# Second layer of a spectral mixture-of-experts kernel: operand addresses of both matrix products moved by 64 bytes

## The chip, the cores and the metric

The kernel runs on one core of a Trainium2 chip. The metric is the device time of one execution in microseconds (us). Three runs of the kernel before gave 3828.07, 3829.45 and 3830.55 us; the median is 3829.45 us.

The core's engines are TensorE (PE in the profile; its weight loads are listed as PEld), VectorE (DVE), ScalarE (ACT), GpSimd (POOL) and SyncE (SP). On-chip memory has 128 partitions, and an address here is the byte at which a tile starts within each partition.

## The reference

```python
# x: (8, 3072, 256); stage 1, a circular convolution along the sequence
X = np.fft.rfft(x, axis=1)
y = np.fft.irfft(X * (filt_r + 1j * filt_i)[None], n=3072, axis=1)
x = y.reshape(24576, 256)
# first layer: 8 experts, each token to its best one
e_idx = np.argmax(x @ w_gate, axis=1)
h = np.maximum(x[mask] @ w1[e], 0.0)              # 256 -> 1024
out[mask] = gate_w * eom * (h @ w2[e])            # 1024 -> 256
# second layer: dense
h = np.maximum(x @ w_in, 0.0)                     # 256 -> 2048
return (h * h) @ w_out                            # 2048 -> 256
```

The change touches the second layer only.

## The kernel before

The kernel runs three stages: the transform with its filter and inverse, the first layer (its matmuls run from 606.5 to 1793.2 us, at first between those of the transform), and the second layer (from 1797.9 us to the end). All engine programs are written out in the order in which the code emits them; waits between engines are semaphores that follow from the data.

A matmul has a stationary operand, which a weight load brings into the array first, and a moving operand, which is streamed through it. In the profile a matmul is written `out<-moving,stationary`.

**Second layer.** The 24576 tokens are 48 tiles of 512. The 2048 inner columns are 8 blocks `u` of 256. One pair (tile, block) is a unit; there are 384. Numbers are split in a high and a low part (`bh`/`bl`, `hh`/`hl`, `wsh`/`wsl`, `woh`/`wol`), and each product is three matmuls: high x high, low x high and high x low.

- `up2` (L881 holds its matmul) forms one block of h. It uses 7 products of 128 x 128 by 128 x 256 in place of 8, so 21 matmuls of 256 columns. Its stationary operands are 128-column pieces of the weights `wsh` and `wsl`, its moving operands the seven pieces of 256 columns of the split tile, `bh` and `bl`. It has four parts with 6, 6, 6 and 3 matmuls.
- ScalarE and VectorE then add up the quarters (`C`, L888 to L903), square the positive part (`q`, L905) and split it into `hh` and `hl` (`split_h`, L912 and L914).
- `down2` (L927) multiplies by the second weights. Here the stationary operands are 128-column pieces of `hh` and `hl`, and the moving ones are rows of 256 columns of `woh` and `wol`. It has 24 matmuls of 256 columns, in four parts with 3, 6, 9 and 6.
- `steps_m` interleaves them: in step n it emits part 0 of `up2` of unit n, part 0 of `down2` of unit n - 2, then part 1 of both, and so on. So a step has 45 matmuls, in which the products change from one to the other eight times. `split_h` of unit n - 1 goes between, and in some steps also a part of `split_t` (L860 to L871), which splits the next tile.

**Where the tiles stand.** `wsh`, `wsl`, `woh` and `wol` are allocated one after the other in the pool `wres` on the left side of the memory; behind it come the pools of the loaded tiles and of the decoder. On the right side `open_m2` opens its pools one below the other, first `pad2`, a tile of 16 floats (64 bytes) that nothing reads. All other tiles have sizes that are multiples of 512 bytes. In the program of the kernel before the tiles start at these bytes:

| tile | first byte | modulo 512 | modulo 128 |
|---|---|---|---|
| wsh, wsl | 21504, 50176 | 0 | 0 |
| woh, wol | 78848, 95232 | 0 | 0 |
| bh (2 buffers), bl (2) | 199616, 206784, 213952, 221120 | 448 | 64 |
| hh (3 buffers), hl (3) | 148416 to 156608, 160704 to 168896 | 448 | 64 |

The pieces within a tile that a matmul takes begin at multiples of 512 bytes, so the last two columns hold for every operand. In the first layer all operands (`xh`, `xl`, `wh`, `wl`, `hh`, `hl` of L802 and L819) start at multiples of 512 bytes.

Of the kernel before, what the change touches and what calls it, by code (L numbers as in the profile page):

```python
# [12 lines left out]
F32 = mybir.dt.float32  # L13
# [89 lines left out]
def spectral_moe_kernel(ctx: ExitStack, tc: tile.TileContext, x, filt_r, filt_i, w_gate, w_og, w1, w2,  # L103
# [58 lines left out]
    pl = {"xsm": ctx.enter_context(tc.tile_pool(name="xsm", bufs=2, side="right"))}  # L162
# [458 lines left out]
    def decode(pool, src, parts, val=None):  # L621


        v = nc.vector
        raw = pool.tile([128, ND, 2], I32, name="raw")
        nc.sync.dma_start(out=raw, in_=src)
        yield
        H, L = raw[:, :, 1], raw[:, :, 0]
        ea = pool.tile([128, ND], I32, name="ea")
        eb = pool.tile([128, ND], I32, name="eb")  # L630
        v.tensor_scalar(ea, H, 20, 0x7FF, op0=ALU.logical_shift_right, op1=ALU.bitwise_and)
        v.tensor_scalar(eb, ea, 896, 0, op0=ALU.subtract, op1=ALU.max)
        v.tensor_scalar(ea, eb, 255, None, op0=ALU.min)
        v.tensor_scalar(eb, ea, 23, None, op0=ALU.logical_shift_left)
        yield
        v.tensor_scalar(ea, H, -2147483648, None, op0=ALU.bitwise_and)
        v.tensor_tensor(eb, ea, eb, ALU.bitwise_or)
        yield
        v.tensor_scalar(ea, H, 0xFFFFF, 3, op0=ALU.bitwise_and, op1=ALU.logical_shift_left)
        mb_ = pool.tile([128, ND], I32, name="mb_")  # L640
        v.tensor_scalar(mb_, ea, 0x3F800000, None, op0=ALU.bitwise_or)
        P = eb.bitcast(F32)
        a = pool.tile([128, ND], F32, name="a")
        v.tensor_tensor(a, mb_.bitcast(F32), P, ALU.mult)
        yield
        v.tensor_scalar(ea, L, 1, None, op0=ALU.logical_shift_right)
        lf = pool.tile([128, ND], F32, name="lf")
        v.tensor_scalar(lf, ea, 2.0 ** -51, None, op0=ALU.mult)
        v.tensor_tensor(lf, lf, P, ALU.mult)
        yield  # L650
        if val is not None:
            v.tensor_tensor(val, a, lf, ALU.add)
        for at, hi, lo in parts:
            v.tensor_tensor(hi, a[:, at], lf[:, at], ALU.add)
            v.tensor_tensor(a[:, at], a[:, at], hi.bitcast(F32), ALU.subtract)
            v.tensor_tensor(lo, a[:, at], lf[:, at], ALU.add)
        yield

    def decode_all():
        wres = ctx.enter_context(tc.tile_pool(name="wres", bufs=1))  # L660


        wsh, wsl = (wres.tile([128, F2 // 256, 7, 128], F32R, name=n) for n in ("wsh", "wsl"))
        woh, wol = (wres.tile([128, F2 // 128, D], F32R, name=n) for n in ("woh", "wol"))
        w2nd.extend((wsh, wsl, woh, wol))
        lpool.append(ctx.enter_context(tc.tile_pool(name="rp2", bufs=2)))
        pool = dcs.enter_context(tc.tile_pool(name="dcp", bufs=1))
        first, second = slice(0, 128), slice(128, 256)
        for u in range(F2 // 256):
            a0, a1 = (pool.tile([128, ND], F32, name=f"val{c}") for c in range(2))  # L670
            for c, val in enumerate((a0, a1)):
                yield from decode(pool, w_in32[c * 128:(c + 1) * 128, 2 * u * ND:2 * (u + 1) * ND]
                                  .rearrange("p (n two) -> p n two", two=2),
                                  [(at, wsh[:, u, i], wsl[:, u, i])
                                   for at, i in (((first, 0),), ((first, 1), (second, 2)))[c]], val)
            sc = pool.tile([128, 4, 128], F32, name="sc")
            v.tensor_tensor(sc[:, 0], a0[:, second], a1[:, second], ALU.add)
            v.tensor_tensor(sc[:, 1], sc[:, 0], a0[:, first], ALU.subtract)
            v.tensor_tensor(sc[:, 2], a0[:, first], a0[:, second], ALU.subtract)
            v.tensor_tensor(sc[:, 3], a1[:, first], sc[:, 1], ALU.subtract)  # L680
            yield
            nc.scalar.copy(wsh[:, u, 3:7], sc)
            v.tensor_tensor(wsl[:, u, 3:7], sc, wsh[:, u, 3:7].bitcast(F32), ALU.subtract)
            yield
        for f in range(F2 // 128):
            yield from decode(pool, w_out32[f * 128:(f + 1) * 128].rearrange("p (d two) -> p d two", two=2),
                              [(slice(0, D), woh[:, f, :], wol[:, f, :])])
# [152 lines left out]

    def open_m2():
        right(ctx, "pad2", 1).tile([128, 16], F32, name="pad2")
        for name, bufs in (("bp", 2), ("tp2", 1), ("sp", 2), ("cp", 2), ("h2p", 3), ("oup", 2)):
            pl[name] = right(ctx, name, bufs)

    def load_t(t):
        r = lpool[0].tile([128, 2, TT], F32, name="r")
        nc.sync.dma_start(out=r, in_=ytd[:, t * TT:(t + 1) * TT].rearrange("(h p) t -> p h t", p=128))
        ix = lpool[0].tile([128, 4], I32, name="ix", bufs=4)
        nc.sync.dma_start(out=ix, in_=idsc[t * TT:(t + 1) * TT, 0:1].rearrange("(c p) o -> p (c o)", p=128))  # L850
        R[t] = r, ix
# [151 lines left out]
    def steps_m():  # L1003
# [15 lines left out]
        m1.close()  # L1019
        xgs.close()  # L1020
        open_m2()
        st = split_t(0)
        for _ in st:
# [95 lines left out]
    tables()  # L1119
    open_left()  # L1120
    dec.append(decode_all())
    for _ in m:
        pass
# [33 lines left out]
```

## Time and profile before

| | |
|---|---|
| median of three runs | 3829.45 us |
| the profiled execution | 3831.18 us |
| its span, first to last instruction | 3829.5 us |
| TensorE busy | 3762.7 us, 98% of the span |
| VectorE busy | 2767.0 us, 72% |
| ScalarE busy | 1973.5 us, 52% |
| GpSimd busy | 608.2 us, 16% |
| granted TensorE clock, mean | 0.994 |

How to read it: matmuls are pipelined, and the duration of one overlaps the next; the pace of the engine is read from the starts. Durations and starts come from the one profiled execution, the median from three others.

### The profile page before, as it was taken

To read this page: it belongs to the slowest core of one execution; us is meant where nothing else is said; L and a number is where in the kernel's file an instruction comes from. 1 tells how busy PE (TensorE), PEld (TensorE's weight loads), DVE (VectorE), ACT (ScalarE), POOL (GpSimd) and SP (SyncE) were. 2 spreads that over 40 slices of the span, in tenths; PEclk is the share of its full clock that TensorE was granted. 3 is DMA by queue.
4 is the path that set the end of the run, shared out by engine and by line. 5 is a ranking of instruction groups with operands and counts; after the bars stand their busy time and mean duration, and the time that the engine had idled before them with its cause. 6 is when DMAs were issued, how large, how long until landed. Compare 5 with 4: busy or idle time off the path is not lost.

```text
span 3829.5 us, 73425 instructions
## 1 busy us (share of the span) xinstructions
PE 3762.7 (98%) x27256; PEld 3512.9 (92%) x27256; DVE 2767.0 (72%) x5038; ACT 1973.5 (52%) x3909; POOL 608.2 (16%) x641
## 2 busy tenths in 40 slices
PE   8999999999999999999999999999999999999998
PEld 7888877788888888888999999999999999999998
DVE  6678685688888866655777777777777777777776
ACT  6466463354545545544555555555555555555554
POOL 3477575000000000000001100100110010011001
PEclk9999999999999999999999999999999999999999
DMA  6333322455555545543010010001001000100100
GB/s 194 100 117 113 105 86 91 142 158 165 170 163 173 178 150 161 164 148 114 23 29 23 29 29 23 29 23 29 23 29 29 23 29 23 29 23 29 29 18 18
DMA packets 262750, 309.30 MB, mean 81 GB/s; under 512 B 75153, under 2 KB 206194, under 8 KB 262386
## 3 DMA queue, kind: packets, MB, share of 16 engines
q1 hardware_dynamic: 242928, 252.39, 21.8%
q0 software_dynamic: 18432, 51.93, 3.8%
q8 instruction: 215, 3.52, 0.4%
q14 instruction: 149, 1.22, 0.1%
q10 hardware_dynamic: 1026, 0.23, 0.0%
HBM read 224.01 MB, written 80.45 MB: 80 GB/s over the span
## 4 chain that ended last, share of the span: by engine, by line
PE 37%; issue 14%; POOL 2%; DVE 0%; ACT 0%; POOLq 0%; DVEq 0%; ACTq 0%
PE py L927 20%; PE ph L881 13%; PE px L881 5%; POOL out_dram L936 2%; DVE tc L867 0%; DVE bl L871 0%; DVE hl L914 0%; DVE bl L861 0%; ACT bh L869 0%; POOLq L1152 0%; DVE C L899 0%; ACT ou L933 0%; ACT bh L860 0%; ACT u L895 0%; DVE C L900 0%
## 5 line engine op out<-in xcount | busy, mean ns | idle before, releaser
L927 PE MATMUL py<-woh,hh 128*128 128x256 f32 x3072 | 857.2, 279 | 0.0
L927 PE MATMUL py<-woh,hl 128*128 128x256 f32 x3072 | 852.8, 278 | 0.4 <-DVE hl L914 0.4
L927 PE MATMUL py<-wol,hh 128*128 128x256 f32 x3072 | 852.9, 278 | 0.0
L936 POOL DMA_INDIRECT out_dram<-ou,ix x192 | 214.0, 1115 | 2935.7 <-ACT ou L933 2891.8
L927 PEld LDWEIGHTS py<-woh,hl 128*128 128x128 f32 x3072 | 579.9, 189 | 0.9 <-DVE hl L914 0.8
L927 PEld LDWEIGHTS py<-woh,hh 128*128 128x128 f32 x3072 | 579.9, 189 | 0.0
L927 PEld LDWEIGHTS py<-wol,hh 128*128 128x128 f32 x3072 | 576.3, 188 | 0.0
L806 ACT ACTIVATE hh<-ph 128x512 fp32r<-128x512 f32 (+1 forms) x472 | 251.8, 533 | 586.3 <-PE ph L802 559.3
L881 PE MATMUL ph<-bh,wsh 128*128 128x256 f32 x1920 | 541.5, 282 | 5.6 <-ACT bh L860 4.4
L881 PE MATMUL ph<-bh,wsl 128*128 128x256 f32 x1920 | 539.2, 281 | 0.0
L881 PE MATMUL ph<-bl,wsh 128*128 128x256 f32 x1920 | 539.0, 281 | 0.0
L905 DVE SCALAR_TENSOR_TENSOR q<-C 128x1024 f32<-128x1024 f32 x384 | 468.3, 1220 | 2.3 <-ACT C L903 2.2
L808 DVE SCALAR_TENSOR_TENSOR hl<-ph,hh 128x512 fp32r<-128x512 f32 (+1 forms) x472 | 286.8, 608 | 253.4 <-ACT hh L806 248.5
L914 DVE TENSOR_TENSOR hl<-q,hh 128x1024 fp32r<-128x1024 f32 x384 | 467.1, 1217 | 1.1 <-ACT hh L912 1.1
L899 DVE TENSOR_TENSOR C<-ph,p 128x256 f32<-128x256 f32 x384 | 163.5, 426 | 417.1 <-ACT hh L912 412.8
L903 ACT COPY C<-ph 128x256 f32<-128x256 f32 x384 | 143.0, 372 | 519.7 <-PE ph L881 518.2
L912 ACT CAST hh<-q 128x1024 fp32r<-128x1024 f32 x384 | 403.1, 1050 | 1.3 <-DVE q L905 1.3
L881 PEld LDWEIGHTS ph<-bh,wsh 128*128 128x128 f32 x1920 | 363.0, 189 | 6.9 <-issue 4.6
L881 PEld LDWEIGHTS ph<-bl,wsh 128*128 128x128 f32 x1920 | 361.6, 188 | 0.0
L881 PEld LDWEIGHTS ph<-bh,wsl 128*128 128x128 f32 x1920 | 361.5, 188 | 0.0
L819 PE MATMUL py<-hh,wh 128*128 128x512 f32 (+1 forms) x944 | 348.4, 369 | 0.0
L802 PE MATMUL ph<-xh,wh 128*128 128x512 f32 (+1 forms) x944 | 340.3, 360 | 0.0
(261 smaller groups left out, 8184.2 us busy)
## 6 DMA issues: line engine op xcount, KB each, us to landing
r<-in_moe_w_dram SPq DMA_DIRECT2D x448, 256.0 KB
xt<-in_x_dram SPq DMA_DIRECT2D x48, 512.0 KB
r<-ytd SPq DMA_DIRECT2D x48, 512.0 KB
xg<-srt SPq DMA_DIRECT2D x41, 544.0 KB
ytd<-yt SPq DMA_DIRECT2D x41, 512.0 KB
xg<-srt SPq DMA_DIRECT2D x18, 272.0 KB
ytd<-yt SPq DMA_DIRECT2D x18, 256.0 KB
raw<-in_moe_w_in_dram SPq DMA_DIRECT2D x16, 256.0 KB
```

Of the source, the lines that this page charges most:

```text
L802: nc.tensor.matmul(ps, a[:, c, f2 * 128:(f2 + 1) * 128], b[:, c, 0:w], start=n == 0, stop=n == 5)
L806: nc.scalar.activation(hh, ps, AF.Relu)
L808: nc.vector.scalar_tensor_tensor(hl, ps, 0.0, hh.bitcast(F32), op0=ALU.max, op1=ALU.subtract)
L819: nc.tensor.matmul(Y[t][h], a[:, f % 2, h * 128:(h + 1) * 128], b, start=f == 0 and i == 0, stop=f == NF - 1 and i == 2)
L881: nc.tensor.matmul(ps, x[:, u, a], y[:, b], start=start and n == 0, stop=n == 2, skip_group_check=True)
L899: nc.vector.tensor_tensor(C[:, 3], V, p5, ALU.add)
L903: nc.scalar.copy(C[:, 2], V)
L905: nc.vector.scalar_tensor_tensor(q, C, 0.0, C, op0=ALU.max, op1=ALU.mult)
L912: nc.scalar.copy(hh, q)
L914: nc.vector.tensor_tensor(hl, q, hh.bitcast(F32), ALU.subtract)
L927: nc.tensor.matmul(Z[t][k][:, c, :], x[:, 2 * i + k, c * 128:(c + 1) * 128], w[:, 2 * u + i, :], start=u == 0 and m in (0, 12), stop=u == ...
L936: nc.gpsimd.indirect_dma_start(out=outv[4 * t + c], out_offset=bass.IndirectOffsetOnAxis(ap=io[:, c:c + 1], axis=0), in_=ou[:, c, :], in_o ...
```

## The change

Two tiles of 16 floats per partition (64 bytes) are allocated that no instruction reads or writes. `wpad` stands between the first weights (`wsh`, `wsl`) and the second ones (`woh`, `wol`); what is allocated behind it on the left side moves up by 64 bytes. `pad3` is a pool of its own, opened between the pool of `C` and `q` and the pool of `hh` and `hl`; what is opened after it on the right side moves down by 64 bytes.

```diff
         wsh, wsl = (wres.tile([128, F2 // 256, 7, 128], F32R, name=n) for n in ("wsh", "wsl"))
+        wres.tile([128, 16], F32, name="wpad")
         woh, wol = (wres.tile([128, F2 // 128, D], F32R, name=n) for n in ("woh", "wol"))
...
         right(ctx, "pad2", 1).tile([128, 16], F32, name="pad2")
-        for name, bufs in (("bp", 2), ("tp2", 1), ("sp", 2), ("cp", 2), ("h2p", 3), ("oup", 2)):
+        for name, bufs in (("bp", 2), ("tp2", 1), ("sp", 2), ("cp", 2), ("pad3", 1), ("h2p", 3), ("oup", 2)):
             pl[name] = right(ctx, name, bufs)
+            if name == "pad3":
+                pl[name].tile([128, 16], F32, name="pad3")
```

By these sizes `woh` and `wol` come to start at 64 modulo 128 and modulo 512, and `hh` and `hl` at 0 modulo 128 (384 modulo 512); `wsh`, `wsl`, `bh` and `bl` stay.

## Rows read from the trace of the kernel before

**Rows 1.** Windows: PE, PEld, DVE, ACT, POOL busy us (count), clock, DMA share, GB/s.
```profile
2500.00:3000.00 500.00, 500.00 (x4302) 500.00 (x4301) 368.49 (x575) 260.28 (x549) 53.65 (x48) 1.00 0.09 27
```

**Rows 2.** Costliest groups: line, engine, operands, shape, count, busy us, mean ns.
```profile
L927 PE MATMUL py<-woh,hh 128*128 128x256 f32 x3072 | 857.2, 279 | 0.0
```

**Rows 3.** Timeline of TensorE (start us, duration us), the layer's 51st and 17233rd matmul.
```profile
1813.30 0.28 PE L927 MATMUL py<-wol,hh 128*128 128x256 f32 x1
...
3812.37 0.28 PE L927 MATMUL py<-woh,hh 128*128 128x256 f32 x1
```

**Rows 4.** Timeline of TensorE over a unit and a half, first matmuls of stretches.
```profile
2801.06 0.28 PE L881 MATMUL ph<-bh,wsh 128*128 128x256 f32 x1
...
2802.12 0.28 PE L881 MATMUL ph<-bh,wsh 128*128 128x256 f32 x1
...
2803.16 0.28 PE L881 MATMUL ph<-bh,wsh 128*128 128x256 f32 x1
...
2804.58 0.28 PE L881 MATMUL px<-bh,wsh 128*128 128x256 f32 x1
...
2805.27 0.28 PE L927 MATMUL py<-woh,hh 128*128 128x256 f32 x1
...
2806.29 0.28 PE L881 MATMUL ph<-bh,wsh 128*128 128x256 f32 x1
...
2808.39 0.28 PE L881 MATMUL ph<-bh,wsh 128*128 128x256 f32 x1
...
2809.81 0.28 PE L881 MATMUL px<-bh,wsh 128*128 128x256 f32 x1
```

**Rows 5.** Timeline, a matmul of L927 and the weight load behind it.
```profile
2800.94 0.28 PE L927 MATMUL py<-wol,hh 128*128 128x256 f32 x1
2800.95 0.19 PEld L881 LDWEIGHTS ph<-bh,wsh 128*128 128x128 f32 x1
```

**Rows 6.** Timeline of TensorE in the first layer, ends of two runs of steps.
```profile
1697.65 0.39 PE L802 MATMUL ph<-xh,wl 128*128 128x512 f32 x1
...
1711.25 0.39 PE L802 MATMUL ph<-xh,wl 128*128 128x512 f32 x1
...
1783.38 0.28 PE L802 MATMUL ph<-xl,wh 128*128 128x256 f32 x1
...
1793.22 0.28 PE L819 MATMUL py<-hh,wl 128*128 128x256 f32 x1
```

**Rows 7.** Timeline of TensorE at the layer's end, where only L927 runs.
```profile
3812.72 0.28 PE L927 MATMUL py<-wol,hh 128*128 128x256 f32 x1
...
3815.31 0.28 PE L927 MATMUL py<-woh,hh 128*128 128x256 f32 x1
3815.97 0.39 PE L927 MATMUL py<-woh,hl 128*128 128x256 f32 x1 [0.38 <-DVE hl L914]
3816.20 0.28 PE L927 MATMUL py<-wol,hh 128*128 128x256 f32 x1
...
3818.67 0.28 PE L927 MATMUL py<-wol,hh 128*128 128x256 f32 x1
```

**Rows 8.** Timeline of TensorE at the layer's start, after a stop in L881.
```profile
1811.61 0.39 PE L881 MATMUL ph<-bh,wsh 128*128 128x256 f32 x1 [0.59 <-DVE C L899]
...
1812.07 0.28 PE L881 MATMUL ph<-bh,wsh 128*128 128x256 f32 x1
...
1812.75 0.28 PE L927 MATMUL py<-woh,hh 128*128 128x256 f32 x1
```

**Rows 9.** Timeline of VectorE in the unit of rows 4.
```profile
2800.31 0.43 DVE L899 TENSOR_TENSOR C<-ph,p 128x256 f32<-128x256 f32 x1 [1.33 <-ACT hh L912]
...
2803.25 1.22 DVE L871 TENSOR_TENSOR bl<-tc,bh 128x1024 fp32r<-128x1024 f32 x1
```

**Rows 10.** Timeline of TensorE where L881 waited for L899.
```profile
2298.36 0.28 PE L927 MATMUL py<-wol,hh 128*128 128x256 f32 x1
...
2298.77 0.28 PE L881 MATMUL ph<-bl,wsh 128*128 128x256 f32 x1
```

## The prediction

> **What bounds the kernel now.** I read the windows first, then the page's costliest groups, then the timeline of TensorE. From 2500 to 3000 us TensorE is busy in every microsecond (4302 matmuls) at full granted clock, VectorE 74% and ScalarE 52%, DMA 9% [rows 1]: the second layer is bound by how fast matmuls follow each other. The chain of waits that ended last says little here (it runs over the scatters of the output), and a matmul's duration (about 280 ns) says nothing either, since they overlap. What counts is the time from the start of one to the start of the next. A unit (one tile of 512 rows and 256 of the 2048 inner columns) has 24 matmuls of the second product, in three groups of 3072 over the layer [rows 2], and by the code 7 x 3 = 21 of the first, so 45 x 384 = 17280 in all. From the 51st to the 17233rd, 17182 steps take 3812.37 - 1813.30 = 1999.07 us, 116.35 ns each [rows 3].
>
> That mean hides two paces. Below, U is the first product (L881) and D the second (L927); a unit changes from D to U four times. Its four stretches from one such change to the next [rows 4]: 9 steps from 2801.06 in 1.06 us (118 ns); 9 from 2802.12 in 1.04 (116); 12 from 2803.16 in 1.42 (118); 15 from 2804.58 in 1.71, of which the six of U at its head take 0.69 (115) and the nine of D after 2805.27 take 1.02 (113.3). So there is a fast pace of 113.3 ns, reached a few steps into every second stretch, and a slow one near 118, and **each change from D to U turns one into the other**; the change from U to D inside each stretch does not. VectorE is not the cause: in the third stretch it runs L871 for 1.22 us [rows 9], which it does in some units only, and the same stretch of the next unit (from 2808.39) takes 1.42 us too.
>
> Why a D-to-U change can matter is in the load rows: the weight load of the next matmul starts 0.01 us after the start of the present one [rows 5] (a D, and the load of the U behind it), so the moving operand of one matmul is read beside the stationary operand of the next. By the addresses (the section on the kernel has them), modulo 128 bytes: inside U the pair is moving 64 / stationary 0, inside D moving 0 / stationary 64; at D to U it is 0 / 0 and at U to D 64 / 64. Equal offsets arise only where the product changes.
>
> The first layer is the cross-check. There all operands stand at 0, and going from one product to the other flips nothing: 60 steps of 512 columns in 13.60 us (226.7 ns each) and 82 steps of 256 columns in 9.84 us (120.0 ns each) pass through both products without a break [rows 6]. So a pace, once taken, lasts while the offsets stay as they are; and 256 columns with equal offsets settle at 120.0, worse than either pace of the second layer.
>
> **The change part by part.** It adds no instruction: two tiles of 16 floats that nothing reads or writes. wpad moves woh, wol, the buffers of the loaded tiles and the decoder's scratch up by 64 bytes; pad3 moves the halves of h and the output buffers down by 64. U keeps moving 64 / stationary 0; D gets moving 64 / stationary 0 as well, and so do both changes of product. The whole layer becomes one row of equal pairs.
>
> Cost of the moves themselves: decoding, the tile loads, the output copies and the split of h run on engines with room (VectorE 74%, ScalarE 52%) [rows 1], with the same shapes; I take zero, bounded by a few ns on an instruction that the matmuls cover. If that cover were gone, it would show as waits of U on VectorE, priced below.
>
> The main term is the pace. Bounds: everything fast, 113.3 ns; everything slow, which the trace shows unmixed at the very end, where D alone runs: 22 steps from 3812.72 to 3815.31 are 2.59 us, 117.7 ns, and it stays so [rows 7]. The sums over 17182 steps: fast 17182 x (116.35 - 113.33) = 51.9 us gained; slow 17182 x (117.7 - 116.35) = 23.2 us lost.
>
> Which one? Two rows speak for fast. After a full stop in U, with exactly the offsets that all pairs get, the stream came down to 113.3 by itself (1811.61 the stop; from 1812.07 six steps in 0.68 us) [rows 8]; that start lies before the first D and does not change. And in this trace the only thing that ever turned fast into slow, apart from a stop, was the D-to-U change with its equal offsets, which goes. Against it: after a stop in D (moving 0, stationary 64), at 3815.97, the stream was slow: 21 steps from 3816.20 to 3818.67 take 2.47 us, 117.6 ns [rows 7]. If the sense of the 64 bytes matters, D now has the sense of U, the good one; if only their being apart matters, a stop is a toss. I take fast.
>
> What is late next: U's last step of a unit adds into a bank that VectorE's L899 must have read. L899 runs from 2800.31 to 2800.74 [rows 9], and TensorE comes at 2801.06 [rows 4]: 0.32 us to spare, behind a D stretch that runs fast already. Where VectorE or ScalarE also splits a new tile, L899 is late now and then: from 2298.36 to 2298.77 two steps take 0.41 us for some 0.23 [rows 10], 0.18 us lost. Two more like it stand in the timeline, near 1932 and 3622 us. The other parts of a unit get some 0.1 us shorter, so more may come: at worst one for each of 48 tiles, 48 x 0.18 = 8.6 us, and nothing at best; I take 1.5 us, near the three of now. Behind the waiting matmul only TensorE's own queue stands, and that is in the price.
>
> The Trainium skill speaks against the whole argument: its page "SBUF — State Buffer", section "Who interferes with whom", gives TensorE two read ports, one for the moving operand and one for the weight load, independent of each other, and says that it never waits on anyone. By that rule offsets cannot change the pace, and the time stays as it was; the pattern of [rows 4] does not agree with it, since the same instruction takes 113 or 118 ns with nothing to wait for.
>
> **Sum.** The profiled execution took 3831.18 us, its span 3829.5; it lies 1.7 us over the median of 3829.45. Profiled: 3831.2 - 51.9 + 1.5 = 3780.8; on the median's footing 3829.45 - 50.4 = 3779.
>
> **Rivals.** *Slow throughout.* The first D matmuls of the layer stop and restart: the first starts at 1812.75 [rows 8], the third at 1813.30 [rows 3], 0.55 us for two steps. If the restart lands in the slow pace, no change of product is left to bring it back: 3829.45 + 23 = 3853. For it: D's restart above was slow, and slow is as lasting as fast. Against it: it had the other sense, and U's restart was fast. It decides as soon as more than about 70% of the steps run slow (3.0 ns gained against 1.35 ns lost per step).
>
> *A mixture.* Fast at first, and a stop (three in the layer, perhaps more) throws it into slow until the next one. Half and half is -51.9/2 + 23.2/2 = -14 us, 3815; between 3790 and 3822 for other shares.
>
> *No change, 3829.* The flip comes with the product whatever the addresses, or the distance counts over more than 128 bytes: over 256, the pairs inside both products become alike (192 ahead), but at a change of product the distance is 64, so something could still flip. Or the pace has another cause than the offsets. Against it: the first layer changes product without a flip. That the pads do not move what they say can be left out: pad2 in the kernel before is the same device, and its 64 bytes stand in the addresses.
>
> **Chances.** Fast throughout 0.56, with its own range 3770 to 3790 (no new waits and a little more gain at the ends; 8.6 us of waits). Mixture 0.14. No change 0.12. Slow throughout 0.18. A measurement of this kernel tells 0.2% (7.7 us) from no change. Faster: 0.56 + 0.14 = 0.70; same 0.12; slower 0.18. The range reaches from 3770 over the mixture and no change to 3836 and leaves out the slow case and a little below.
>
> **What would show it.** Right: steps of 113.3 ns through all four D-to-U changes of a unit, some 4410 matmuls in 500 us where there were 4300, a unit of 5.10 us; the three stops still there. Slow throughout: some 4250 in 500 us. No change: 118 and 113 still alternate at D to U. Wrong altogether: a third pace under 113 or at 120, or U's waits on VectorE growing past 10 us.

## The result, and the profile after

The change made the kernel slower, by less than 1% but clear of the noise: median 3856.38 us (four runs, 3853.92 to 3859.14) against 3830.0 us (four runs, 3828.07 to 3832.10). The ratio is 1.0069, with a 95% interval of 1.0052 to 1.0086. The forecast was 3779 us. The profiled execution took 3856.74 us, with a span of 3855.0.

In the changed kernel U stands at L884 and D at L930; the other lines of the second layer are three further down as well (L899 is L902).

Windows of the kernel after, in the stretch and the columns of [rows 1]:

```profile
2500.00:3000.00 500.00, 500.00 (x4243) 500.00 (x4242) 365.85 (x568) 258.23 (x543) 50.30 (x45) 1.00 0.09 26
```

TensorE is still busy all the time at full clock, but 500 us hold 4243 matmuls where they held 4302. The prediction named 4410 for its forecast, 4250 for "slow throughout" and 4300 for "no change".

Timeline of TensorE after (start us, duration us), the layer's 51st and 17233rd matmul, as in [rows 3]:

```profile
1811.39 0.28 PE L930 MATMUL py<-wol,hh 128*128 128x256 f32 x1
...
3837.96 0.28 PE L930 MATMUL py<-woh,hh 128*128 128x256 f32 x1
```

These 17182 steps take 2026.57 us, 117.95 ns each, where they took 116.35: 17182 x 1.60 ns = 27.5 us lost. The layer's steady part starts 1.9 us earlier than before, and the tail behind it is 0.1 us shorter (17.0 against 17.1 us). So 27.5 - 1.9 - 0.1 = 25.5 us, which is the whole difference of the spans (3855.0 - 3829.5). The pace is the whole loss. The page's busy times do not tell it: the costliest group of TensorE stays at about 280 ns a matmul, as in [rows 2].

```profile
L930 PE MATMUL py<-woh,hh 128*128 128x256 f32 x3072 | 863.0, 281 | 0.0
```

Timeline of TensorE after, one unit, the first matmul of each stretch, as in [rows 4]:

```profile
2395.50 0.28 PE L884 MATMUL ph<-bh,wsh 128*128 128x256 f32 x1
...
2396.21 0.28 PE L930 MATMUL py<-woh,hh 128*128 128x256 f32 x1
...
2396.92 0.28 PE L884 MATMUL px<-bh,wsh 128*128 128x256 f32 x1
...
2397.62 0.28 PE L930 MATMUL py<-woh,hh 128*128 128x256 f32 x1
...
2398.69 0.28 PE L884 MATMUL ph<-bh,wsh 128*128 128x256 f32 x1
...
2399.04 0.28 PE L930 MATMUL py<-woh,hh 128*128 128x256 f32 x1
...
2399.75 0.28 PE L884 MATMUL ph<-bh,wsh 128*128 128x256 f32 x1
...
2400.46 0.28 PE L930 MATMUL py<-woh,hh 128*128 128x256 f32 x1
...
2400.81 0.28 PE L884 MATMUL ph<-bh,wsh 128*128 128x256 f32 x1
```

The stretches have 6, 6, 6, 9, 3, 6, 6 and 3 matmuls; each takes 117 to 119 ns a step, U and D alike, and the unit 5.31 us. The alternation of [rows 4] is gone, but so is its fast half. Averaged step by step over 188 units between 2500 and 3500 us, the 45 steps repeat one pattern. A stretch behind one that had come down to 114 ns stays at 117 to 119 ns up to its next change of product; three of the eight do so, the one with nine of D among them. In the other five the pace comes down, to 116 and 114 ns by the sixth step, or to 115 by the third where there are only three, and the next change throws it up again. So this is not one lasting slow pace. As before, the pace turns at changes of product, up or down, but now at all eight of them, and the fast pace is hardly reached before the next change.

That the pair itself can run fast shows where nothing changes any more. Timeline of TensorE after, the layer's end with D alone (where [rows 7] had 117.7 ns):

```profile
3838.28 0.28 PE L930 MATMUL py<-wol,hh 128*128 128x256 f32 x1
...
3838.98 0.28 PE L930 MATMUL py<-wol,hh 128*128 128x256 f32 x1
...
3840.79 0.28 PE L930 MATMUL py<-woh,hh 128*128 128x256 f32 x1
```

The first 6 steps take 0.70 us (117 ns), the next 16 take 1.81 us (113 ns). The restart in U at the layer's head is as fast as in [rows 8]; timeline of the same kernel:

```profile
1810.16 0.28 PE L884 MATMUL ph<-bh,wsh 128*128 128x256 f32 x1
...
1810.84 0.28 PE L930 MATMUL py<-woh,hh 128*128 128x256 f32 x1
```

Six steps in 0.68 us. And the three stops of [rows 10], places where U has to wait for VectorE, are there, about as long as they were; timeline of the same kernel:

```profile
2302.91 0.28 PE L930 MATMUL py<-wol,hh 128*128 128x256 f32 x1
2303.06 0.38 PE L884 MATMUL ph<-bh,wsh 128*128 128x256 f32 x1
2303.28 0.28 PE L884 MATMUL ph<-bl,wsh 128*128 128x256 f32 x1
```

Two steps take 0.37 us, some 0.14 more than without a stop, where [rows 10] lost 0.18; the other two stand near 1931 and 3646 us.

### The profile page after: what moved, and what is told of

It reads as the page before. It is cut to its first block, busy times and chain, and to the rows that moved or that the text cites. A ratio compares the mean times of both kernels' runs of the same rounds, so it can differ in the third digit from the quotient of the medians.

```text
span 3855.0 us, 73425 instructions
## 1 busy us (share of the span) xinstructions
PE 3788.5 (98%) x27256; PEld 3538.8 (92%) x27256; DVE 2768.4 (72%) x5038; ACT 1978.2 (51%) x3909; POOL 606.9 (16%) x641
## 4 chain that ended last, share of the span: by engine, by line
PE 52%; issue 1%; DVE 0%; POOL 0%; ACT 0%; POOLq 0%; ACTq 0%; DVEq 0%
PE py L930 28%; PE ph L884 17%; PE px L884 7%; POOL out_dram L939 0%; DVE tc L870 0%; DVE bl L874 0%; DVE hl L917 0%; POOLq L1155 0%; DVE bl L864 0%; ACT bh L872 0%; DVE C L902 0%; ACT bh L863 0%; ACT u L898 0%; DVE C L903 0%; DVEq L902 0%
## 5 line engine op out<-in xcount | busy, mean ns | idle before, releaser
L930 PE MATMUL py<-woh,hl 128*128 128x256 f32 x3072 | 864.6, 281 | 0.5 <-DVE hl L917 0.5
L930 PE MATMUL py<-woh,hh 128*128 128x256 f32 x3072 | 863.0, 281 | 0.0
L930 PE MATMUL py<-wol,hh 128*128 128x256 f32 x3072 | 862.2, 281 | 0.0
L930 PEld LDWEIGHTS py<-woh,hh 128*128 128x128 f32 x3072 | 583.4, 190 | 0.0
L930 PEld LDWEIGHTS py<-woh,hl 128*128 128x128 f32 x3072 | 576.8, 188 | 0.9 <-DVE hl L917 0.9
L930 PEld LDWEIGHTS py<-wol,hh 128*128 128x128 f32 x3072 | 577.1, 188 | 0.0
L884 PE MATMUL ph<-bh,wsh 128*128 128x256 f32 x1920 | 541.1, 282 | 5.8 <-ACT bh L863 4.6
L884 PE MATMUL ph<-bl,wsh 128*128 128x256 f32 x1920 | 540.4, 281 | 0.0
L884 PE MATMUL ph<-bh,wsl 128*128 128x256 f32 x1920 | 536.0, 279 | 0.0
L902 DVE TENSOR_TENSOR C<-ph,p 128x256 f32<-128x256 f32 x384 | 163.1, 425 | 427.6 <-PE ph L884 419.6
L884 PEld LDWEIGHTS ph<-bh,wsh 128*128 128x128 f32 x1920 | 363.4, 189 | 7.0 <-issue 4.8
L884 PEld LDWEIGHTS ph<-bh,wsl 128*128 128x128 f32 x1920 | 362.0, 189 | 0.0
L884 PEld LDWEIGHTS ph<-bl,wsh 128*128 128x128 f32 x1920 | 361.7, 188 | 0.0
```

Of the source, the lines that this page charges most:

```text
L884: nc.tensor.matmul(ps, x[:, u, a], y[:, b], start=start and n == 0, stop=n == 2, skip_group_check=True)
L902: nc.vector.tensor_tensor(C[:, 3], V, p5, ALU.add)
L930: nc.tensor.matmul(Z[t][k][:, c, :], x[:, 2 * i + k, c * 128:(c + 1) * 128], w[:, 2 * u + i, :], start=u == 0 and m in (0, 12), stop=u == ...
```

## The experiments

**The theories.** Counted modulo 256 instead of 128, the change does not make the layer one row of equal pairs. The addresses (moving / stationary) are:

| kernel | U | D | at a change of product |
|---|---|---|---|
| before | 192 / 0 | 0 / 192 | both operands move by 64 |
| after | 192 / 0 | 64 / 128 | both operands jump by 128 |

Theory A: addresses count modulo 256 bytes, and a jump of the operands between two products disturbs the stream; without a jump, a pace lasts. (A jump is a difference, modulo 256, between the bytes at which the operands of U and of D start.) The rivals: the change of product disturbs by itself, whatever the addresses; the other tiles that the two pads moved are the cause; the place 64 / 0 (modulo 128) is a bad one for D. Further theories of the pair came in with later runs: N stands for "operands that start alike modulo 128 run at 120 ns" and O for "the distance counts modulo 256, so operands 128 apart run at 113 or 118 ns".

All edits below are against the changed kernel. "Pace" is the mean over the 17182 steps of the profiled execution. The runs fall on three chips, on which the kernel before took 3834.0, 3821.4 and 3819.8 us, so each is compared by its ratio to the kernel before on its own chip.

**No jump: D's operands brought to U's offsets.** Once modulo 512 (`e1_same512`), once only modulo 256 (`e2_same256`): U and D both at 192 / 0.

```diff
 # e1_same512
-        wres.tile([128, 16], F32, name="wpad")
+        wres.tile([128, 112], F32, name="wpad")
...
-                pl[name].tile([128, 16], F32, name="pad3")
+                pl[name].tile([128, 112], F32, name="pad3")
 # e2_same256: 48 floats in the place of 112, in both
```

> Both pads of 448 bytes in place of 64: the second product's operands start at the same bytes modulo 512 as the first's (moving 448, stationary 0). Theory A (a change of product disturbs the pace because the operands jump within 256 or 512 bytes; without a jump the stream settles at 113.3 ns): all steps 113.3 ns also at the changes, 17182 x (117.95 - 113.33) = 79 us less than the changed kernel's 3856, so about 3778. Rival B (the change of product itself disturbs once the second product stands at moving 64 / stationary 0 modulo 128): 117.9 ns as before, 3856. Rival C (the tiles moved along, output buffers, decoder's scratch and the halves of h, collide with VectorE or ScalarE): 3856 as well, with no reason for 113.3.

> Both pads of 192 bytes: the second product's operands equal the first's modulo 256 (moving 192, stationary 0), but modulo 512 they differ by 256. Theory A with a period of 256 bytes: 113.3 ns throughout, 3778. Theory A with a period of 512: the changes still disturb, pace 116 to 118 ns, 3825 to 3856. Rivals B and C: 3856.

Measured: e2 3780.08 us, ratio 0.9867 (0.9851 to 0.9884), pace 113.40. e1 spread from 3780.01 to 3838.25 over four runs (median 3809.96); the trace of one of them, below, is a mixture of two paces, and for a spread like this neither a median nor a ratio says much. Windows of e1, TensorE alone (busy us and count, clock, DMA share, GB/s):

```profile
1830.00:1900.00 70.00, 70.00 (x620) 1.00 0.07 24
2500.00:3000.00 500.00, 500.00 (x4248) 1.00 0.08 27
3650.00:3740.00 90.00, 90.00 (x797) 1.00 0.06 22
```

70 us / 620 and 90 / 797 are about 113 ns, 500 / 4248 is 117.7: two paces, each lasting for hundreds of microseconds through every change of product. What stands between them is a stop. Timeline of TensorE in e1:

```profile
2281.68 0.28 PE L930 MATMUL py<-wol,hh 128*128 128x256 f32 x1
2281.88 0.38 PE L884 MATMUL ph<-bh,wsh 128*128 128x256 f32 x1
...
2282.33 0.28 PE L930 MATMUL py<-woh,hh 128*128 128x256 f32 x1
...
2283.04 0.28 PE L884 MATMUL ph<-bh,wsh 128*128 128x256 f32 x1
...
2283.75 0.28 PE L930 MATMUL py<-woh,hh 128*128 128x256 f32 x1
```

From the stop at 2281.7 on, six steps of D and six of U take 0.71 us each (118 ns); the stop near 3622 brings the fast pace back. The size fits: some 1340 us at 117.78 are 11,380 steps, at 4.45 ns too many 50.6 us, and 3826.97 (e1's profiled execution) - 50.6 = 3776.4, e2's having taken 3776.95. In e2 the same stops left the fast pace as it was until 3745 us, where a fourth one made the last 13 us slow. Windows of e2:

```profile
2500.00:3000.00 500.00, 500.00 (x4414) 1.00 0.09 28
```

What follows: with no jump there is no disturbance at any of the changes of product, though the products alternate as ever. That takes away the rival "the change of product itself". In e2 the operands of U and D differ by 256 bytes modulo 512, and that is as good as no difference: to start alike modulo 256 is enough.

**One jump alone.** `e6_moving_same` leaves only the stationary jump (U 192 / 0, D 192 / 128), `e7_stationary_same` only the moving one (U 192 / 0, D 64 / 0).

```diff
 # e6_moving_same
-        wres.tile([128, 16], F32, name="wpad")
+        wres.tile([128, 112], F32, name="wpad")
 # e7_stationary_same
-                pl[name].tile([128, 16], F32, name="pad3")
+                pl[name].tile([128, 112], F32, name="pad3")
```

> wpad of 448 bytes, pad3 of 64: the moving operands of both products start alike modulo 512 (448), the stationary ones differ (0 and 384). Theory A, if a jump of the moving operand is what disturbs: 113.3 ns, 3778. Theory A, if a jump of the stationary operand disturbs: still kicked at every change, 116 to 118 ns, 3825 to 3856. Rivals B and C: 3856.

> wpad of 64 bytes, pad3 of 448: the stationary operands of both products start alike modulo 512 (0), the moving ones differ (448 and 64). Theory A, if a jump of the moving operand disturbs: kicked at every change, 116 to 118 ns, 3825 to 3856. Theory A, if a jump of the stationary operand disturbs: 113.3 ns, 3778. Rivals B and C: 3856.

Measured: e6 3778.91 us (3777.05 to 3781.00), ratio 0.9864 (0.9848 to 0.9881), pace 113.39. e7 3834.37 us, ratio 1.0004 (0.9994 to 1.0014), pace 116.60. Windows of e6 and then of e7:

```profile
1830.00:1900.00 70.00, 70.00 (x620) 1.00 0.08 24
2500.00:3000.00 500.00, 500.00 (x4414) 1.00 0.09 28
3650.00:3740.00 90.00, 90.00 (x797) 1.00 0.05 16
```

```profile
2500.00:3000.00 500.00, 500.00 (x4301) 1.00 0.08 27
```

Timeline of TensorE in e7, first matmuls of stretches:

```profile
2705.45 0.28 PE L884 MATMUL ph<-bh,wsh 128*128 128x256 f32 x1
...
2706.13 0.28 PE L930 MATMUL py<-woh,hh 128*128 128x256 f32 x1
...
2706.49 0.28 PE L884 MATMUL ph<-bh,wsh 128*128 128x256 f32 x1
...
2707.17 0.28 PE L930 MATMUL py<-woh,hh 128*128 128x256 f32 x1
...
2707.88 0.28 PE L884 MATMUL px<-bh,wsh 128*128 128x256 f32 x1
```

U takes 0.68 us for 6 steps, twice; D takes 0.36 for 3 and 0.71 for 6. So the moving jump alone throws the stream into the slow pace going to D and back into the fast one going to U, and the mean is that of before by another pattern. (After its stop at 1930 us e7 ran some 370 us at 117.78 without any such turn, up to the next stop.) The stationary jump alone leaves a fast stream fast, and does more: timeline of TensorE in e6 around a stop:

```profile
2282.57 0.28 PE L930 MATMUL py<-wol,hh 128*128 128x256 f32 x1
2282.76 0.38 PE L884 MATMUL ph<-bh,wsh 128*128 128x256 f32 x1
...
2283.23 0.28 PE L930 MATMUL py<-woh,hh 128*128 128x256 f32 x1
...
2283.93 0.28 PE L884 MATMUL ph<-bh,wsh 128*128 128x256 f32 x1
...
2284.61 0.28 PE L930 MATMUL py<-woh,hh 128*128 128x256 f32 x1
2284.95 0.28 PE L884 MATMUL ph<-bh,wsh 128*128 128x256 f32 x1
```

After the stop six steps of D take 0.70 us (slow), but from the next change to U on six take 0.68 and three 0.34. All four stops of e6 (1925, 2283, 3573 and 3746 us) heal like this, at a change from D to U and within some 20 steps. Theory A in its first form (any jump disturbs) is too wide: of the two jumps alone, the moving operand's costs and the stationary one's does not. But alone the moving jump leaves the kernel as fast as before (ratio 1.0004). The 117.95 ns of the changed kernel come only with both jumps, and why the stationary jump, which heals in e6, adds 1.35 ns to e7's mean there is not shown. Nor is it the distance within a pair: counted from the stationary operand up to the moving one it is 192 in U and 64 in D in both kernels, and at a change it is one of the same two values, yet e6 runs through and e7 turns.

**Half of the change.** `e3_wpad_only` keeps `wpad` (U 192 / 0, D 64 / 192), `e4_pad3_only` keeps `pad3` (U 192 / 0, D 0 / 128).

```diff
 # e3_wpad_only: without pad3
-        for name, bufs in (..., ("cp", 2), ("pad3", 1), ("h2p", 3), ("oup", 2)):
+        for name, bufs in (..., ("cp", 2), ("h2p", 3), ("oup", 2)):
-            if name == "pad3":
-                pl[name].tile([128, 16], F32, name="pad3")
 # e4_pad3_only: without wpad
-        wres.tile([128, 16], F32, name="wpad")
```

> The first half of the change alone: wpad of 64 bytes, no pad3. Modulo 256 the first product stands at moving 192 / stationary 0, the second at moving 64 / stationary 192. Theory A (the jump of the moving operand at a change of product, here 128 modulo 256 as in the whole change, disturbs; pairs that are equal modulo 128 settle at 120 ns): second product 120 ns, first 117 to 118, mean 118.8, 17182 x (118.8 - 116.35) = 42 us over the kernel before, 3872. Rival D (equal offsets count modulo 256 only): as in the whole change, 3856. Rival E (the wpad is the harmless half): 3830.

> The second half alone: pad3 of 64 bytes, no wpad. Modulo 256 the first product stands at 192 / 0, the second at moving 0 / stationary 128. The moving operand jumps by 64 as in the kernel before. Theory A: second product 120 ns (equal modulo 128), mean about 118.5, 3867. Rival D: as the kernel before, 3830. Rival F (pad3 is what slows the whole change, through the tiles that move with it): 3856.

Measured: e3 3850.17 us, ratio 1.0075 (1.0058 to 1.0092), pace 118.10; e4 3840.04 us, ratio 1.0052 (1.0035 to 1.0069), pace 117.51. Theory A's numbers (3872 and 3867, ratios of 1.011 and 1.010) were missed by both. e3 meets the number of rival D, the ratio of the whole change, but D's other number, no change for e4, was missed; e4 lies between D's number and F's (1.0069), which its interval just touches, and F's reason goes with e6, which keeps `pad3` and is fast. Both halves slow the kernel, and they do not add up to the whole (1.0069). In both D's operands are 128 apart, which by itself has a price of its own (e9 below), so these two runs do not tell the jump from the pair.

**The pair without a jump.** `e8_first_moved` leaves D where the change puts it modulo 128 and brings U there too, alike modulo 256: both at 64 / 0. `e5_all_zero` takes all pads out: both at 0 / 0, as in the first layer. `e9_distance128` has both at 128 / 0, `e10_distance32` both at 224 / 0, 32 bytes apart.

```diff
 # e8_first_moved
-        right(ctx, "pad2", 1).tile([128, 16], F32, name="pad2")
+        right(ctx, "pad2", 1).tile([128, 48], F32, name="pad2")
 # e5_all_zero: without wpad, pad2 and pad3
 # e9_distance128:  wpad 96, pad2 32, pad3 96 floats
 # e10_distance32:  wpad 120, pad2 8, pad3 120 floats
```

> The changed kernel with pad2 of 192 bytes in place of 64: now the first product moves to the second (both moving 64 / stationary 0 modulo 256), the reverse of the runs before; modulo 512 they differ by 256 in the stationary operand alone. Theory A: no kick at the changes; 113.3 ns, or 117.8 from one stop to the next, so 3778 to 3855, likeliest 3778. Rival H (the second product at 64 / 0 is itself the bad place): 117.9 ns, 3856, with the pattern of the changed kernel.

> No pad at all, pad2 of the kernel before left out as well: all operands of both products start at multiples of 512 bytes, as in the first layer. No jumps at the changes. Theory A: every step 120.0 ns as the steps of 256 columns in the first layer, 17182 x (120.0 - 116.35) = 63 us more, 3893, and no change of pace at the changes of product. Rival G (only jumps matter, not the distance of the two operands): 113.3 or 117.8 ns, 3778 or 3855.

> All moving operands at 384 modulo 512 (128 modulo 256), all stationary ones at 0: the two operands are equal modulo 128 but not modulo 256, and nothing jumps. Theory N (within a pair the distance counts modulo 128): 120.0 ns, about 63 us over the kernel before. Rival O (it counts modulo 256): 113.3 or 117.8 ns, 52 us under to 24 us over.

> All moving operands at 480 modulo 512, all stationary ones at 0: they are 32 bytes apart in place of 64, and nothing jumps. If only being apart by some line matters: 113.3 or 117.8 ns as with 64 (52 us under to 24 us over the kernel before). If 32 bytes is not apart: 120 ns, 63 us over. A pace under 113.3 ns would show that 113.3 is not the floor of these matmuls.

| kernel | both products at | pace, ns | time, us | ratio (95%) |
|---|---|---|---|---|
| e8 | 64 / 0 | 117.54 | 3842.40 | 1.0058 (1.0042 to 1.0075) |
| e5 | 0 / 0 | 120.02 | 3879.83 | 1.0161 (1.0144 to 1.0178) |
| e9 | 128 / 0 | 118.70 | 3857.27 | 1.0098 (1.0081 to 1.0116) |
| e10 | 224 / 0 | 118.36 | 3855.59 | 1.0094 (1.0077 to 1.0111) |

Windows of TensorE, of e8, e5, e9 and e10 in this order:

```profile
1830.00:1900.00 70.00, 70.00 (x620) 1.00 0.09 26
2500.00:3000.00 500.00, 500.00 (x4247) 1.00 0.08 26
```

```profile
2500.00:3000.00 500.00, 500.00 (x4169) 1.00 0.08 26
```

```profile
2500.00:3000.00 500.00, 500.00 (x4216) 1.00 0.09 26
```

```profile
2500.00:3000.00 500.00, 500.00 (x4228) 1.00 0.08 26
```

e8 is fast (620 matmuls in 70 us, as e1 and e6) until this stop, and at 117.78 from there to the end, past two more stops; timeline of TensorE in e8:

```profile
1914.67 0.39 PE L884 MATMUL ph<-bh,wsh 128*128 128x256 f32 x1
...
1915.13 0.28 PE L930 MATMUL py<-woh,hh 128*128 128x256 f32 x1
...
1915.84 0.28 PE L884 MATMUL ph<-bh,wsh 128*128 128x256 f32 x1
```

So 64 / 0 is no bad place for D: up to the stop it runs at 113.33 with no turn at a change. The loss is what the stop left. Whether that is chance is not shown: all four runs of e8 are slow (3837.63 to 3843.38 us), where all four of e2 were fast. The rival "the moved tiles" goes too: e8 keeps the tiles on the left side where the changed kernel has them, e6 those on the right side, and both ran at 113.3 ns through the changes, so that neither group alone is the cause. Offsets that are equal cost 120.0 on every step, which confirms the reading of the first layer in [rows 6]; 128 and 32 bytes apart give neither lasting pace, but steps that wander between 114 and 123 ns. So 128 apart is neither N's 120.0 nor O's lasting 113.3 or 117.8. Of the distances run without a jump (0, 32, 64 and 128 bytes), only 64 reached a lasting 113.3.

**The two fast kernels again, on another chip.** The edits are those of e2 and e6.

> Both pads of 192 bytes once more: nothing jumps modulo 256. Theory L (a stretch between two stops keeps the pace that the stop left it with): executions fall into steps, all fast 51 us under the kernel before, or up to 24 us over it where the long stretches are slow, as the run with 448 bytes did (3780 to 3838). Rival M (at these offsets every stop ends fast): all executions 50 to 53 us under.

> wpad of 448 bytes and pad3 of 64 once more, with more rounds: moving operands alike (192 modulo 256), stationary ones jump by 128 at each change of product. Theory J (this jump turns slow into fast and leaves fast alone, so that the layer comes back to 113.3 ns after each stop): every execution 50 to 53 us under the kernel before, with a spread no wider than its own. Rival K (the four runs before were lucky draws at the stops): some executions lie up to 75 us higher.

Measured: e6b 3767.85 us (four runs, 3766.11 to 3771.59) against 3819.83: ratio 0.9863 (0.9848 to 0.9877). e2b: three runs took 3765.90 to 3768.24 and nine 3814.58 to 3833.42; the median of the twelve, 3818.76, is no faster than the kernel before. Windows of e2b's profiled execution (3833.42 us) and of e6b's:

```profile
1830.00:1900.00 70.00, 70.00 (x620) 1.00 0.07 24
2500.00:3000.00 500.00, 500.00 (x4247) 1.00 0.08 26
3650.00:3740.00 90.00, 90.00 (x797) 1.00 0.06 19
```

```profile
2500.00:3000.00 500.00, 500.00 (x4414) 1.00 0.09 27
```

e2b is the kernel e2, and here it is fast, then slow from the stop at 1917 us to that at 3629, then fast. Its three good runs are as fast as e6b. That bears out theory L against M: a layer without any jump keeps what its last stop left it with. For e6, J stands and K does not: with its stationary jump it came out fast in all eight runs on two chips. e6 is the version that beats both kernels, by 1.36% against the kernel before.

## Why the prediction was wrong

- **What bounds the layer:** right. The loss of 25.5 us is the steps' pace (27.5) less an earlier start (1.9) and a shorter tail (0.1); no new wait for an engine or a transfer took part.
- **"So a pace, once taken, lasts while the offsets stay as they are":** right, with one limit that [rows 7] had already shown at the layer's end: a stop can change it. e1, e2b and e8 show both paces lasting through hundreds of units, and the turn at a stop. e5 shows the 120.0 ns of equal offsets.
- **"The whole layer becomes one row of equal pairs":** this step failed. It counted addresses modulo 128. Modulo 128 the change does what its words say; modulo 256, D stands 128 bytes from U in both operands, and every change of product, in both directions, now turns the pace: 117.95 ns a step, and not 113.3. Where the operands of both products agree modulo 256 (e1, e2, e8), no change of product does anything. With this step fell the reason given for the turns before, the equal offsets at a change from D to U: in the changed kernel no change of product brings equal offsets together, counted modulo 128 or 256, and all eight turn. The prediction had the period of 256 as half a sentence under "no change" ("at a change of product the distance is 64, so something could still flip") and took the time of before for it, without working out what a disturbance at all eight changes instead of four turns would cost. By that sentence's own distances e6 should have turned as well; of the jumps run alone, it is the moving operand's that turns the pace (e7).
- **Fast as the pace of the pair itself:** right as far as it goes: D alone at the end of the layer now settles at 113 ns where it had stayed at 117.7, and e2 and e6 ran at 113.40 and 113.39 over the whole layer, forecast 113.33. A gain like the 50.4 us forecast was there to be had (e6: 55.1 and 52.0 us on two chips), for other addresses.
- **"Slow throughout", 3853:** near in number (3856) by luck, and not what happened. Its mechanism is a lasting 117.7 ns from one bad restart, as e8 shows it; in the changed kernel the pace keeps turning, and slow stretches alternate with ones that come down to 114 or 115 ns.
- **The mixture:** not in the changed kernel, but it is what decides e1, e2b and e8. The prediction gave it 0.14 and tied it to the stops, and there it belongs.
- **The term of the stops (1.5 us on top of those of before):** nothing was added; three stops, about as long as they were, which lies at the lower of the bounds stated (nothing to 8.6). L902 does not become the bound. In e2, e6 and their like, though, a stop's own 0.2 us is nothing beside the 50 us that it can decide.

Still open: why two paces 4.45 ns apart both last, where the period of 256 bytes comes from, why the stationary jump turns slow into fast when it is alone and adds to the cost when the moving operand jumps too, and what decides the pace behind a stop. No run has both products at e6's place of D (192 / 128), so that place and the jump are not told apart in its healing. That of the two jumps alone the moving one costs is shown for a jump of 128 from 192 / 0; other sizes were not run alone, and the turns of the kernel before, with jumps of 64, at the changes from D to U only, are not explained.

## What to carry to other kernels

Where a stream of short matmuls is all that bounds a stage, read its pace from the starts and compare it over stretches; if it has two values without a wait, list where every operand begins and try the offsets of moving and stationary operands before anything else, with pads that no instruction touches. Work out such an argument modulo every period that the trace does not exclude, since here 128 and 256 differ in the sign of the result. And repeat a fast version: without any jump the same program took 3766 us in one run and 3833 in another, and of the two kernels run again only e6 was fast every time.

## What was unexpected in the hardware

Streams of matmuls of 256 columns that did not wait for data took 113.3, 116 to 118.7 or 120.0 ns a step, with the same instructions and only pads between them: the kernel takes 3778.91 us at the offsets of e6, 0.9864 of the kernel before on the same chip, and 3879.83 at those of e5, 1.0161 of it. At some offsets a stop of 0.2 us or so chose between 113.3 and 117.8 ns for more than 1000 us. No run had a lasting pace under 113.3 ns.

The Trainium skill's page "SBUF — State Buffer", section "Who interferes with whom", says that TensorE reads moving operand and weights over two independent ports and never waits on anyone. By that, offsets should make no difference, and these runs do not agree: at full granted clock and with TensorE busy all the time, 500 us held 4414 matmuls in e6 and 4169 in e5. Where the difference arises, at the ports or elsewhere, no run shows.
